# Group normalisation in 32 tiles: the next tile's mean read ahead of this tile's variance on VectorE

## The chip, the cores and the metric

The kernel runs on one core of a Trainium2 chip. The metric is the device time of one execution in microseconds (us). Times quoted are medians of several executions. One core gives no second core to compare with, so "fast" below means only that an execution lay within 1.5% of the fastest of its kernel. The span of a profile is the time from its first to its last instruction; it is some 1.7 us shorter than the device time.

## The reference

```python
# x: (128, 1024, 32, 16) bf16; g, b: (1024,) bf16; 32 groups of 32 channels
xr  = x.reshape(B, 32, 32, H, W)
mu  = xr.mean(axis=(2, 3, 4), keepdims=True)
var = ((xr - mu) ** 2).mean(axis=(2, 3, 4), keepdims=True)
xn  = (xr - mu) / sqrt(var + 1e-5)
return xn.reshape(B, C, H, W) * g[None, :, None, None] + b[None, :, None, None]
```

The input has 134 MB and so has the output. Both pass through the DMA once.

## The kernel before

A row of a tile is one group of one sample: 32 channels of 512 elements. A tile is 128 such rows, 4 MiB; there are 32 tiles and six buffers for them. Loads and stores all go out on one queue. For each tile `i`:

- `L(i)` loads it; `M(i)` has TensorE add up its 32 slices with an identity matrix, into PSUM (the memory that TensorE writes its sums to);
- `R(i)` reads those sums on VectorE and makes the (negative) mean;
- `Q(i)` squares the tile, less its mean, in four passes on ScalarE, each with a sum;
- `V(i)` makes variance, 1/sqrt, scale and bias: small VectorE steps with one ScalarE square root among them;
- `A(i, lo, hi)` scales slices `lo` to `hi` in place on VectorE, one instruction each;
- `S(i)` stores it.

```python
def chain(key, inst):            # keeps the instructions of one engine in program order
    prev = last.get(key)
    if prev is not None:
        tc.add_manual_dep(inst.ins, prev.ins.name, nosync, reason="pipeline order")
    last[key] = inst
    return inst

# ... (constants; the casts of gamma and beta on VectorE, which are in no chain)

def R(i):                        # mean of tile i: waits for M(i)
    ...
    chain("dve", nc.vector.tensor_scalar(out=jd[:], in0=st["ps"][:], scalar1=-inv_n, ...,
                                         accum_out=negmean[:]))

def V(i):                        # ... four VectorE steps and this one on ScalarE:
    chain("act", nc.scalar.activation(out=rstd[:], in_=var[:], func=ACT.Sqrt, bias=eps_t[:], ...))

# ...
M(0)
R(0)
for i in range(NT):
    Q(i)
    V(i)
    if i + 1 < NT:
        M(i + 1)
    A(i, 0, A_HEAD)              # A_HEAD = 12 of 32 slices
    if i + 1 < NT:
        R(i + 1)                 # the next mean stands between two parts of the scaling
    A(i, A_HEAD, KC)
    S(i)
    j = i + AHEAD                # AHEAD = 5; L(j) reuses the buffer of tile i-1
    if UPFRONT <= j < NT:
        L(j)
```

Of the kernel before, what the change touches and what calls it, by code (L numbers as in the profile page):

```python
# [18 lines left out]
AHEAD = 5  # L19
MM_FREE = 512  # L20
SQ_FREE = 4096
A_HEAD = 12


@with_exitstack
def kernel(
# [16 lines left out]
    NT = B0 // NS  # L43
    KC = C // G
# [25 lines left out]
    def chain(key, inst):  # L70
# [5 lines that stand above are left out]
# [3 lines left out]
    def L(i):  # L79
        xt = xpool.tile([P, F], BF16, name="xt")  # L80
        chain("sp", nc.sync.dma_start(out=xt[:], in_=x_v[i]))
        state[i] = {"xt": xt}
# [32 lines left out]
    def M(i):  # L115
        st = state[i]
        ps = pspool.tile([P, MMN], F32, name="ps")
        for k in range(NMM):
            chain(
                "pe",  # L120
                nc.tensor.matmul(  # L121
                    out=ps[:],
                    lhsT=eye[:],
                    rhs=st["xt"][:, k * MMN : (k + 1) * MMN],
                    start=(k == 0),
                    stop=(k == NMM - 1),
                ),
            )
        st["ps"] = ps

    def R(i):
        st = state[i]
        negmean = spool.tile([P, 1], F32, name="negmean")
        jd = jpool.tile([P, MMN], BF16, name="jd")
        chain(
            "dve",
            nc.vector.tensor_scalar(  # L137
                out=jd[:],
                in0=st["ps"][:],
                scalar1=-inv_n,  # L140
                scalar2=None,
                op0=ALU.mult,
                op1=ALU.add,
                accum_out=negmean[:],
            ),
        )
        st["negmean"] = negmean

    def Q(i):
        st = state[i]  # L150
        sq = spool.tile([P, NSQ], F32, name="sq")
        for k in range(NSQ):
            ja = jpool.tile([P, SQ_FREE], BF16, name="ja")
            chain(
                "act",
                nc.scalar.activation(  # L156
                    out=ja[:],
                    in_=st["xt"][:, k * SQ_FREE : (k + 1) * SQ_FREE],
                    func=ACT.Square,
                    bias=st["negmean"][:],  # L160
                    scale=1.0,
                    accum_out=sq[:, k : k + 1],
                ),
            )
        st["sq"] = sq

    def V(i):
        st = state[i]
        var = spool.tile([P, 1], F32, name="var")
        jv = spool.tile([P, NSQ], F32, name="jv")  # L170
        chain(
            "dve",
            nc.vector.tensor_scalar(  # L173
                out=jv[:],
                in0=st["sq"][:],
                scalar1=inv_n,
                scalar2=None,
                op0=ALU.mult,
                op1=ALU.add,
                accum_out=var[:],  # L180
            ),
        )
        rstd = spool.tile([P, 1], F32, name="rstd")
        chain(
            "act",
            nc.scalar.activation(  # L186
                out=rstd[:], in_=var[:], func=ACT.Sqrt, bias=eps_t[:], scale=1.0
            ),
        )
        chain("dve", nc.vector.reciprocal(out=rstd[:], in_=rstd[:]))  # L190
        scl = spool.tile([P, KC], F32, name="scl")
        bia = spool.tile([P, KC], F32, name="bia")
        chain(
            "dve",
            nc.vector.tensor_scalar(  # L195
                out=scl[:], in0=gam[:], scalar1=rstd[:], scalar2=None, op0=ALU.mult
            ),
        )
        chain(
            "dve",  # L200
            nc.vector.scalar_tensor_tensor(  # L201
                out=bia[:],
                in0=scl[:],
                scalar=st["negmean"][:],
                in1=bet[:],
                op0=ALU.mult,
                op1=ALU.add,
            ),
        )
        st["scl"], st["bia"] = scl, bia  # L210

    def A(i, lo, hi):
        st = state[i]
        xt = st["xt"]
        for k in range(lo, hi):
            chain(
                "dve",
                nc.vector.tensor_scalar(  # L218
                    out=xt[:, k * HW : (k + 1) * HW],
                    in0=xt[:, k * HW : (k + 1) * HW],  # L220
                    scalar1=st["scl"][:, k : k + 1],
                    scalar2=st["bia"][:, k : k + 1],
                    op0=ALU.mult,
                    op1=ALU.add,
                ),
            )

    def S(i):
        chain("sp", nc.sync.dma_start(out=o_v[i], in_=state[i]["xt"][:]))
        state.pop(i)  # L230
# [2 lines left out]
    R(0)  # L233
    for i in range(NT):
        Q(i)
        V(i)
        if i + 1 < NT:
            M(i + 1)
        A(i, 0, A_HEAD)
        if i + 1 < NT:  # L240
            R(i + 1)
        A(i, A_HEAD, KC)
        S(i)
        j = i + AHEAD
        if UPFRONT <= j < NT:
            L(j)
# [30 lines left out]
```

## Time and profile before

| | before |
|---|---|
| time | 732.8 us (732.75 to 732.81, 3 runs) |
| ScalarE, VectorE, TensorE busy | 68%, 52%, 40% |
| one tile after another | every 21.28 us |
| bytes moved, both ways | 367 GB/s over the span |

The page of the kernel before. The first row is the busy share of the DMA in 40 slices of the span, in tenths; the second what it moved; then the chain that ended last (the work followed back from the last instruction, at each step to what released it), by engine.

```profile
DMA  9998599999999999999999999999999999934555
GB/s 377 431 437 364 229 385 390 403 402 377 397 404 402 373 402 401 402 375 402 402 374 402 402 402 372 403 402 402 373 420 385 378 400 398 401 145 202 229 229 229
...
ACT 68%; DVE 25%; DMA 4%; issue 1%; ACTq 0%; DVEq 0%
```

The DMA seems full for 35 slices, but for a dip at the fifth and sixth, and half empty for the last five. Yet the chain hardly runs through it. The waits say why (engine, what it was about to do, for whom it waited: us in all, times, longest):

```profile
DVE jv L173 <- ACT ja L156: 293.1, 32, 15.4
ACT ja L156 <- DVE jd L137: 199.1, 32, 30.1
```

ScalarE's squares (`ja`) wait for VectorE's mean (`jd`), and VectorE's variance (`jv`) waits for ScalarE's squares. That is a loop. The timeline shows one turn of it; each row has start, duration, engine and operation, and in brackets the idle time before it and who ended it.

```profile
303.12 0.16 DVE L173 TENSOR_SCALAR_CACHE_REDUCE jv<-sq 128x4 f32<-128x4 f32 x1 [8.96 <-ACT ja L156]
...
304.41 3.97 DVE L218 TENSOR_SCALAR xt<-xt,scl,bia 128x512 bf16<-128x512 bf16 x12
308.29 0.68 DVE L137 TENSOR_SCALAR_CACHE_REDUCE jd<-ps 128x512 bf16<-128x512 f32 x1
...
309.07 3.71 ACT L156 ACTIVATE ja<-xt,negmean 128x4096 bf16<-128x4096 bf16 x1 [5.46 <-DVE jd L137]
...
324.40 0.16 DVE L173 TENSOR_SCALAR_CACHE_REDUCE jv<-sq 128x4 f32<-128x4 f32 x1 [8.96 <-ACT ja L156]
```

Squares take 15.3 us, the variance steps 1.3, twelve slices 3.97, the mean 0.75: together about 21.3 us, and the turn from 303.12 to 324.40 is 21.28. In each turn ScalarE idles 5.46 us and VectorE 8.96. No engine is full. The Trainium skill ("Perfetto Trace Analysis", Optimization Strategy) has one look for the gaps and for what ends them; here that names the loop at once, where the busy shares name nothing.

Windows in time show that the DMA follows the loop (columns: window, its length, then busy us and number of instructions for PE, PEld, DVE, ACT and POOL, then the TensorE clock, the DMA's busy share and GB/s):

```profile
300.00:400.00 100.00, 40.78 (x149) 15.94 (x146) 58.69 (x194) 71.16 (x42) 0.00 (x0) 0.72 0.96 396
...
645.00:656.00 11.00, 0.59 (x3) 0.10 (x1) 10.91 (x34) 6.44 (x3) 0.00 (x0) 0.75 0.00 0
656.00:666.00 10.00, 0.00 (x0) 0.00 (x0) 0.71 (x5) 9.06 (x7) 0.00 (x0) 0.50 0.98 419
666.00:677.00 11.00, 0.00 (x0) 0.00 (x0) 10.96 (x35) 6.17 (x3) 0.00 (x0) 0.50 0.01 1
```

In the middle it is busy 0.96 of the time; near the end a store takes 10 us and is followed by 11 us of nothing.

### The profile page before, as it was taken

The numbers are of one execution on the slowest core, as the hardware profiler recorded it, in microseconds if no ns is written. First come the engines' busy times: TensorE is split into PE (matmuls) and PEld (weight loads), VectorE is DVE, ScalarE is ACT, GpSimd is POOL, SyncE is SP. The second block draws the span as 40 slices with busy tenths as digits, with TensorE's granted clock in tenths as the row PEclk, the third lists the DMA queues.
The fourth block names the chain that finished last, engine by engine and source line by source line (L and its number), as shares of the span: only waits on it lengthen the run. The fifth ranks groups of instructions, "written<-read, shape, count | busy, mean of one in ns | idle before, by whom it ended". The sixth has DMA issues, their size and how long they took to land.

```text
span 731.1 us, 3814 instructions
## 1 busy us (share of the span) xinstructions
PE 288.9 (40%) x1024; PEld 113.1 (15%) x1024; DVE 379.8 (52%) x1252; ACT 497.5 (68%) x290; POOL 0.5 (0%) x5
## 2 busy tenths in 40 slices
PE   2874532455543334445323455433344443330000
PEld 0331110122111111112111122111111111110000
DVE  0034466654446665444566544456654445665443
ACT  0267876666787666678766667876666787666670
POOL 0000000000000000000000000000000000000000
PEclk9997656666667667776667766677767776675555
DMA  9998599999999999999999999999999999934555
GB/s 377 431 437 364 229 385 390 403 402 377 397 404 402 373 402 401 402 375 402 402 374 402 402 402 372 403 402 402 373 420 385 378 400 398 401 145 202 229 229 229
DMA packets 9622, 268.70 MB, mean 368 GB/s; under 512 B 1408, under 2 KB 1408, under 8 KB 1408
## 3 DMA queue, kind: packets, MB, share of 16 engines
q1 hardware_dynamic: 9216, 268.44, 88.7%
q8 instruction: 8, 0.13, 0.1%
q14 instruction: 14, 0.11, 0.0%
q10 hardware_dynamic: 384, 0.02, 0.0%
HBM read 134.23 MB, written 134.22 MB: 367 GB/s over the span
## 4 chain that ended last, share of the span: by engine, by line
ACT 68%; DVE 25%; DMA 4%; issue 1%; ACTq 0%; DVEq 0%
ACT ja L156 67%; DVE xt L218 18%; DVE jd L137 3%; DMA bet_b<-in_b_dram 3%; DMA xt<-in_x_dram 2%; ACT rstd L186 1%; DVE bia L201 1%; DVE scl L195 1%; DVE jv L173 1%; DVE rstd L190 1%; ACTq L156 0%; DVEq L272 0%; DVE bet L113 0%
## 5 line engine op out<-in xcount | busy, mean ns | idle before, releaser
L156 ACT ACTIVATE ja<-xt,negmean 128x4096 bf16<-128x4096 bf16 x128 | 474.7, 3708 | 202.2 <-DVE jd L137 199.1
L121 PE MATMUL ps<-xt,eye 128*128 128x512 bf16 x1024 | 288.9, 453 | 356.7 <-DMA xt<-in_x_dram 343.9
L218 DVE TENSOR_SCALAR xt<-xt,scl,bia 128x512 bf16<-128x512 bf16 x1024 | 335.9, 403 | 1.2
L121 PEld LDWEIGHTS <-eye 128*128 128x128 bf16 x1024 | 113.1, 113 | 532.0 <-DMA xt<-in_x_dram 343.4
L173 DVE TENSOR_SCALAR_CACHE_REDUCE jv<-sq 128x4 f32<-128x4 f32 x32 | 5.0, 157 | 293.1 <-ACT ja L156 293.1
L156 ACT ACTIVATION_READ_ACCUMULATOR ja<-xt,negmean 128x1 f32 x128 | 23.9, 187 | 0.0
L137 DVE TENSOR_SCALAR_CACHE_REDUCE jd<-ps 128x512 bf16<-128x512 f32 x32 | 21.8, 680 | 0.0
L186 ACT ACTIVATE rstd<-var,eps_t 128x1 f32<-128x1 f32 x32 | 9.4, 294 | 7.4 <-DVE jv L173 7.4
L112 DVE CAST gam<-gam_b 128x32 f32<-128x32 bf16 x1 | 0.2, 181 | 26.9 <-DMA gam_b<-in_g_dram 26.9
L190 DVE RECIPROCAL rstd<-rstd 128x1 f32<-128x1 f32 x32 | 5.3, 164 | 11.6 <-ACT rstd L186 11.6
L201 DVE SCALAR_TENSOR_TENSOR bia<-scl,negmean,bet 128x32 f32<-128x32 f32 x32 | 8.0, 251 | 1.1
L195 DVE TENSOR_SCALAR scl<-gam,rstd 128x32 f32<-128x32 f32 x32 | 7.7, 242 | 1.1
L173 DVE DVE_READ_ACCUMULATOR jv<-sq 128x1 f32 x32 | 2.6, 83 | 0.0
L137 DVE DVE_READ_ACCUMULATOR jd<-ps 128x1 f32 x32 | 2.5, 79 | 0.0
L113 DVE CAST bet<-bet_b 128x32 f32<-128x32 bf16 x1 | 0.2, 181 | 3.4 <-DMA bet_b<-in_b_dram 3.4
L90 ACT ACT_TABLE_LOAD x1 | 1.3, 1283 | 0.8 <-PEq L261 0.8
L88 DVE MEMSET eps_t<- 128x1 f32 x1 | 0.1, 59 | 0.9 <-PEq L261 0.9
L101 POOL TENSOR_SCALAR_AFFINE_SELECT eye<-ones_b 128x128 bf16<-128x128 bf16 x1 | 0.3, 293 | 0.7 <-DVE ones_b L99 0.7
L90 ACT ACTIVATE warm<-eps_t 128x1 f32<-128x1 f32 x1 | 0.2, 202 | 0.0
L99 DVE MEMSET ones_b<- 128x128 bf16 x1 | 0.2, 165 | 0.0
L261 POOL MEMSET const-bfloat16-1.0<- 128x1 bf16 x1 | 0.1, 101 | 0.0
L261 POOL MEMSET const-uint8-127<- 128x1 uint8 x1 | 0.1, 101 | 0.0
(2 smaller groups left out, 0.2 us busy)
## 6 DMA issues: line engine op xcount, KB each, us to landing
xt<-in_x_dram SPq DMA_DIRECT2D x32, 4096.0 KB, 21.9
out_dram<-xt SPq DMA_DIRECT2D x32, 4096.0 KB, 12.1
gam_b<-in_g_dram ACTq DMA_DIRECT2D x4, 2.0 KB, 15.7
bet_b<-in_b_dram ACTq DMA_DIRECT2D x4, 2.0 KB, 17.1
```

The lines of the kernel that those rows point to most:

```text
L90: chain("act", nc.scalar.activation(out=warm[:], in_=eps_t[:], func=ACT.Sqrt))
L99: nc.vector.memset(ones_b[:], 1.0)
L101: nc.gpsimd.affine_select(out=eye[:], in_=ones_b[:], pattern=[[-1, P]], compare_op=ALU.is_equal, fill=0.0, base=0, channel_multiplier=1,)
L121: nc.tensor.matmul(out=ps[:], lhsT=eye[:], rhs=st["xt"][:, k * MMN : (k + 1) * MMN], start=(k == 0), stop=(k == NMM - 1),),
L137: nc.vector.tensor_scalar(out=jd[:], in0=st["ps"][:], scalar1=-inv_n, scalar2=None, op0=ALU.mult, op1=ALU.add, accum_out=negmean[:],),
L156: nc.scalar.activation(out=ja[:], in_=st["xt"][:, k * SQ_FREE : (k + 1) * SQ_FREE], func=ACT.Square, bias=st["negmean"][:], scale=1.0, acc ...
L173: nc.vector.tensor_scalar(out=jv[:], in0=st["sq"][:], scalar1=inv_n, scalar2=None, op0=ALU.mult, op1=ALU.add, accum_out=var[:],),
L186: nc.scalar.activation(out=rstd[:], in_=var[:], func=ACT.Sqrt, bias=eps_t[:], scale=1.0),
L190: chain("dve", nc.vector.reciprocal(out=rstd[:], in_=rstd[:]))
L195: nc.vector.tensor_scalar(out=scl[:], in0=gam[:], scalar1=rstd[:], scalar2=None, op0=ALU.mult),
L201: nc.vector.scalar_tensor_tensor(out=bia[:], in0=scl[:], scalar=st["negmean"][:], in1=bet[:], op0=ALU.mult, op1=ALU.add,),
L218: nc.vector.tensor_scalar(out=xt[:, k * HW : (k + 1) * HW], in0=xt[:, k * HW : (k + 1) * HW], scalar1=st["scl"][:, k : k + 1], scalar2=st[ ...
```

## The change

The intent: ScalarE shouldn't wait for VectorE's scaling. The next tile's mean depends only on its load and its matmuls, so it can be read while ScalarE squares this tile and VectorE is idle. `R(i + 1)` moves ahead of `V(i)`; with nothing left to put between two parts of the scaling, a tile is scaled in one go. No instruction is added or removed.

```diff
-A_HEAD = 12
...
-    def A(i, lo, hi):
+    def A(i):
...
-        for k in range(lo, hi):
+        for k in range(KC):
...
     for i in range(NT):
         Q(i)
-        V(i)
         if i + 1 < NT:
             M(i + 1)
-        A(i, 0, A_HEAD)
-        if i + 1 < NT:
             R(i + 1)
-        A(i, A_HEAD, KC)
+        V(i)
+        A(i)
         S(i)
```

## The prediction

> **What bounds the kernel now.** A loop of waits between two engines, with the DMA close behind. The timeline (300 to 350 us) repeats every 21.28 us: ScalarE squares a tile in four passes (15.3 us), VectorE makes its variance, scale and bias (1.3), scales 12 of 32 slices (3.97), only then reads the next tile's mean (0.7), and that mean releases ScalarE. The waits view shows ScalarE idle 199.1 us for that mean, 32 times, about 5.5 us each and 30 the first time. The chain that ended last says the same: ACT 68%, DVE 25%. No engine is full: ACT 68%, DVE 52%, PE 40%. Loads arrive about two tiles early; PE's 343.9 us of waits for loads are run-ahead.
>
> The DMA moves 8.39 MB per tile. In one-us windows a pair (store, then load) is under way for about 20.2 of the 21.28 us, then nothing for 1.1 to 1.2 us until the next store is issued. In the tail (from 645 us) stores come every 21.28 us and the DMA is idle half the time.
>
> **What the change does.** No instruction is added or removed. The mean of tile i+1 is read while ScalarE squares tile i, when VectorE sits idle 9 us. Removed from the loop: 3.97 us of scaling, 0.7 of mean, and the scale and bias. What is left between two squares is the variance wait (0.23) and the square root (0.3). ScalarE could then do a tile in 15.9 us; VectorE needs 12.5, PE about 8.7.
>
> So the limit passes to the DMA. A transfer of 4.19 MB takes about 9.8 us (six loads at the start land 9.8 apart, mostly), and a pair 20.2. The Trainium skill ("DMA: Bandwidth & Descriptors", Queues, rings and completion order) says that one engine's ring is consumed in order; the trace agrees (store lands 12.1 us after issue, the load behind it 21.9). Its specifications give about 358 GB/s as a core's HBM limit; this trace holds 394 for hundreds of us, so I use the trace.
>
> **Where the gain comes from** (estimates from these durations):
> - Start: store 1 goes out at 75.5 us, not 81.4, and ends an idle DMA: 6 us.
> - Middle: 26 pairs at 20.2 instead of 21.28: about 28 us. ScalarE first gains on the loads, uses up their lead by about tile 11, and then waits for them, so its gain stops there.
> - Tail: the last five stores queue back to back, about 10 us apart, not 21.28: about 45 us.
>
> Sum: DMA starts at 76; 26 pairs x 20.2 = 525; five stores x 9.8 = 49; landing 1.5; launch 1.7. That is 653. I add a few us for load-to-store turnarounds, which before never met back to back: **657 us, 643 to 682**. Chances: faster by over 2% 0.96, within 2% 0.03, slower 0.01.
>
> **Cost of the move.** The variance of tile i now stands behind the mean of i+1 in VectorE's order, so it waits for load i+1. Once loads are late, store i can't go before load i+1 is in. Five tiles of lookahead should hide this; I give it nothing.
>
> **What would show it right.** ScalarE's waits for the mean: near zero for the first 10 tiles, then about 4.5 us each, for the load and the matmuls behind it. Store issues 15.9 us apart at first, then about 20.2. DMA share near full from 76 us to the end, 410 to 420 GB/s; no half-idle tail. Busy times of ACT and DVE unchanged. Chain: mostly DMA.
>
> **What would make it wrong.** Stores and loads really overlapping might run slower (400 GB/s gives about 675), or turnarounds cost 1 us each. If the coupling of store i to load i+1 starves the DMA queue, the middle stays near 21 us and only start and tail pay: about 685.

## The result, and the profile after

| | before | after |
|---|---|---|
| time | 732.77 us (4 runs) | 643.48 us (642.11 to 644.48, 4 runs) |
| ratio | | 0.878 (0.8763 to 0.8797) |
| ScalarE, VectorE, TensorE busy | 68%, 52%, 40% | 77%, 59%, 44% |
| bytes moved over the span | 367 GB/s | 419 GB/s |

A ratio is the mean time of one kernel's fast runs over that of the other's of the same rounds, so it isn't quite the ratio of the medians. The page after:

```profile
DMA  9999699999999999999999999999999999999986
GB/s 370 442 430 425 297 392 424 424 427 433 438 426 427 434 441 417 426 436 439 421 432 431 439 425 427 434 434 429 429 436 438 426 429 436 435 429 427 435 345 270
...
DMA 63%; ACT 22%; PE 8%; DVE 5%; issue 1%; DVEq 0%; SPq 0%
```

The chain now runs through the DMA. The half-empty tail has gone, and the middle moves 431 GB/s (windows below) where it moved 396. The waits that answer to the loop (`L155` and `L136` are the same squares and mean; line numbers moved):

```profile
ACT rstd L185 <- DVE jv L172: 90.1, 32, 4.9
...
ACT ja L155 <- DVE jd L136: 30.0, 1, 30.0
```

ScalarE waits for a mean only once, at the very start. It still waits, for 90.1 us, but under another name: its square root (`rstd`) waits for the variance of its own tile. The timeline shows the reason:

```profile
415.04 8.82 PE L120 MATMUL ps<-xt,eye 128*128 128x512 bf16 x32 [11.59 <-DMA xt<-in_x_dram]
...
423.89 0.69 DVE L136 TENSOR_SCALAR_CACHE_REDUCE jd<-ps 128x512 bf16<-128x512 f32 x1 [8.08 <-PE ps L120]
...
424.51 0.15 DVE L172 TENSOR_SCALAR_CACHE_REDUCE jv<-sq 128x4 f32<-128x4 f32 x1
...
424.70 0.29 ACT L185 ACTIVATE rstd<-var,eps_t 128x1 f32<-128x1 f32 x1 [4.92 <-DVE jv L172]
```

The variance (424.51) stands behind the next tile's mean (423.89), which waits for that tile's matmuls, which waited for its load. So the wait that the trace gives to VectorE comes from the DMA, three steps back.

```profile
300.00:400.00 100.00, 48.56 (x167) 18.98 (x169) 59.29 (x195) 78.47 (x46) 0.00 (x0) 0.71 1.00 431
400.00:500.00 100.00, 47.70 (x162) 18.62 (x165) 59.27 (x195) 78.07 (x46) 0.00 (x0) 0.71 1.00 431
```

The windows of after have the DMA full for hundreds of us. A load is now issued every 19.70 us (187.91 to 562.26 us in the timeline of issues, 19 steps).

Where the 89.7 us of the two traces' spans came from, cut at two marks that both have: the issue of the second store (the first moment from which the changed DMA is never empty for long), and the start of the last tile's matmuls (its load is in):

| | before | after | gained | predicted |
|---|---|---|---|---|
| start to the issue of store 1 | 81.4 | 75.1 | 6.3 | 6 |
| to the last load in | 555.5 | 517.2 | 38.3 | 28 |
| to the end | 94.2 | 49.1 | 45.1 | 45 |
| sum | 731.1 | 641.4 | 89.7 | 79, less 4 of margin |

The third row starts at these rows of the timelines, the first two before, the others after; they show where ScalarE was when the last load was in, and how the changed kernel ends:

```profile
628.25 3.71 ACT L156 ACTIVATE ja<-xt,negmean 128x4096 bf16<-128x4096 bf16 x1 [5.45 <-DVE jd L137]
636.87 8.73 PE L121 MATMUL ps<-xt,eye 128*128 128x512 bf16 x32 [12.64 <-DMA xt<-in_x_dram]
...
581.85 3.69 ACT L155 ACTIVATE ja<-xt,negmean 128x4096 bf16<-128x4096 bf16 x1
592.25 3.17 PE L120 MATMUL ps<-xt,eye 128*128 128x512 bf16 x7 [11.45 <-DMA xt<-in_x_dram]
601.25 0.69 DVE L136 TENSOR_SCALAR_CACHE_REDUCE jd<-ps 128x512 bf16<-128x512 f32 x1 [8.09 <-PE ps L120]
602.26 3.69 ACT L155 ACTIVATE ja<-xt,negmean 128x4096 bf16<-128x4096 bf16 x1
617.58 0.16 DVE L172 TENSOR_SCALAR_CACHE_REDUCE jv<-sq 128x4 f32<-128x4 f32 x1 [4.00 <-ACT ja L155]
618.87 10.42 DVE L217 TENSOR_SCALAR xt<-xt,scl,bia 128x512 bf16<-128x512 bf16 x32
```

### The profile page after: what moved, and what is told of

It reads as the page before. It is cut to its first block, busy times and chain, and to the rows that moved or that the text cites. A ratio compares the mean times of both kernels' runs of the same rounds, so it can differ in the third digit from the quotient of the medians.

```text
span 641.4 us, 3795 instructions
## 1 busy us (share of the span) xinstructions
PE 285.3 (44%) x1004; PEld 112.8 (18%) x1024; DVE 380.2 (59%) x1252; ACT 494.1 (77%) x290; POOL 0.5 (0%) x5
## 4 chain that ended last, share of the span: by engine, by line
DMA 63%; ACT 22%; PE 8%; DVE 5%; issue 1%; DVEq 0%; SPq 0%
DMA out_dram<-xt 30%; DMA xt<-in_x_dram 29%; ACT ja L155 21%; PE ps L120 8%; DVE xt L217 3%; DMA bet_b<-in_b_dram 3%; DVE jd L136 1%; DVE jv L172 0%; ACT rstd L185 0%; DVE scl L194 0%; DVE bia L200 0%; DVE rstd L189 0%; DVEq L269 0%; DVE bet L112 0%; SPq L80 0%
## 5 line engine op out<-in xcount | busy, mean ns | idle before, releaser
L155 ACT ACTIVATE ja<-xt,negmean 128x4096 bf16<-128x4096 bf16 x128 | 474.2, 3704 | 33.1 <-DVE jd L136 30.0
L120 PE MATMUL ps<-xt,eye 128*128 128x512 bf16 x1004 | 285.3, 451 | 315.9 <-DMA xt<-in_x_dram 302.7
L136 DVE TENSOR_SCALAR_CACHE_REDUCE jd<-ps 128x512 bf16<-128x512 f32 x32 | 22.0, 689 | 156.7 <-PE ps L120 149.0
L185 ACT ACTIVATE rstd<-var,eps_t 128x1 f32<-128x1 f32 x32 | 9.4, 294 | 90.1 <-DVE jv L172 90.1
L155 ACT ACTIVATION_READ_ACCUMULATOR ja<-xt,negmean 128x1 f32 x128 | 23.8, 186 | 0.0
L136 DVE DVE_READ_ACCUMULATOR jd<-ps 128x1 f32 x32 | 2.6, 82 | 0.0
```

What stands on the lines that cost most here:

```text
L120: nc.tensor.matmul(out=ps[:], lhsT=eye[:], rhs=st["xt"][:, k * MMN : (k + 1) * MMN], start=(k == 0), stop=(k == NMM - 1),),
L155: nc.scalar.activation(out=ja[:], in_=st["xt"][:, k * SQ_FREE : (k + 1) * SQ_FREE], func=ACT.Square, bias=st["negmean"][:], scale=1.0, acc ...
```

## The experiments

Three questions were open. Is the loop, and its exit behind twelve slices, really what was cured (e1, e2)? Are the three rows of that table three separate gains (e3, e4)? And is the DMA the new limit, and what does a pair of store and load cost on it (e5 to e7)? Then four runs tried to use the answer.

### e1: no slice before the mean, but the mean still behind the variance

```diff
-A_HEAD = 12
+A_HEAD = 0
```

> The old order with the first part of the scaling cut from 12 slices to 0: the next mean is read after the variance but before any slice is scaled. Theory A (what mattered was getting the mean out from behind the 12 slices; after that the DMA limits): the engine loop is 15.3+1.3+0.75, about 17.4 us, shorter than the 19.5 us that a store and a load take, so the time is that of the changed kernel within 1%: 641 to 649 us. Rival B (the mean must also stand ahead of the variance, because the 1.6 us of loop left over counts): 31 x 1.6 = 50 us slower than the changed kernel, about 690 us.

Measured: 645.44 us, ratio 0.881 to before (0.8796 to 0.8825). Theory A holds. Ordering the mean ahead of the variance, which the change is named for, isn't what earns the gain. Taking it out from behind the slices is. In e1 ScalarE waits 111.4 us for means and 7.4 us for variances; the changed kernel has it the other way (30.0 and 90.1). Its waits:

```profile
ACT ja L156 <- DVE jd L137: 111.4, 32, 30.1
...
ACT rstd L186 <- DVE jv L173: 7.4, 32, 0.2
```

The sum is nearly the same, 118.8 and 120.1 us: e1's own loop is longer (its early stores are 17.28 us apart, those of the changed kernel 15.7), but that only takes from the time that ScalarE would otherwise wait for loads. The one difference left that I see is at the start: store 1 leaves at 77.2 us and not 75.1, and the whole is 2.0 us longer.

### e2: six slices before the mean

```diff
-A_HEAD = 12
+A_HEAD = 6
```

> The old order with 6 slices before the next mean. If the loop between ScalarE and VectorE is what bounded the kernel before, its period is 21.28 - 6 x 0.327 = 19.3 us, and as that is near the DMA's 19.5 us the whole is about 670 us (660 to 680), with stores about 19.4 us apart all the way to the end. If the DMA alone had set the 21.28 us, nothing would change in the middle: 715 to 733 us.

Measured: 672.64 us, ratio 0.918 (0.9166 to 0.9194). Stores leave every 19.34 us (311.39 to 582.22 us, 14 steps), up to the last. The loop was the bound of the kernel before: six slices less take 1.94 us off each turn, as estimated (6 x 0.327), and 31 turns of that are 60.1 us, the whole gain. Here the loop's 19.34 us and the DMA's 19.7 are nearly level, yet the kernel is 29 us slower than the changed one. The next two runs say why.

### e3 and e4: the new order in the last tiles only, and everywhere but there

```diff
     for i in range(NT):
         Q(i)
+        if NEW(i):                    # e3: i >= 27    e4: i < 27
+            if i + 1 < NT:
+                M(i + 1)
+                R(i + 1)
+            V(i)
+            A(i, 0, KC)
+        else:
+            ...                       # the old order
```

> The new order for tiles 27 to 31 only (after the last load is issued), the old order before. Theory A (the long tail of the kernel before is a backlog of 3 to 4 loaded but unsquared tiles; the new order saves 5.4 us for each of them, only four steps are left): about 711 us. Rival B (the sum of the prediction, where the tail by itself is worth 45 us): about 688 us.

> The new order for tiles 0 to 26, the old order for 27 to 31. Theory A (the middle drains the backlog, so no long tail is left whichever order it runs in): 645 to 652 us. Rival B (terms add; the tail's 45 us are lost): about 688 us.

Measured: e3 710.45 us (ratio 0.9696, 0.9682 to 0.971), e4 648.80 us (0.8854, 0.8841 to 0.8868). Both fit theory A and both rule out the sum. Fixing only the tail wins 22.3 us of the 45 in the table's third row. Fixing everything but the tail wins 83.9 of 89. So the rows show where the time was seen to go, not what each part is worth alone.

The tail of the kernel before was a backlog. When the last load was in, at 636.9 us, ScalarE was still in the squares of tile 28 (begun at 628.25 us), with 29, 30 and 31 to come, at 21.28 us each. In the changed kernel the last load was in at 592.3 us and ScalarE was in tile 30 (begun at 581.85 us). The faster middle had let ScalarE catch up with the loads, and with no backlog there is no tail to speed up. In e2 the loop runs about as fast as the DMA, so ScalarE hardly catches up: when the last load was in, at 595.4 us, it was in the squares of tile 29, and the rest took 75.6 us and not 49.1. Those 26.5 us are most of its 29.

### e5: the transfers alone

All compute is taken out, and stores and loads keep their order (a wrong result).

```diff
     for i in range(NT):
-        Q(i)
-        ...
-        A(i)
         S(i)
         j = i + AHEAD
         if UPFRONT <= j < NT:
             L(j)
```

> All 32 loads and 32 stores in the same order on the same queue with no compute between (a wrong result on purpose: the input comes out). If the DMA bounds the changed kernel's middle, this takes 64 transfers x 9.75 to 9.85 plus about 5 us: 628 to 640 us, and its pair of store and load takes 19.5 to 19.7 us, as in the changed kernel (425 to 433 GB/s). If the changed kernel's middle is set by something else (ScalarE, PE), it is much shorter: below 600 us.

Measured (one run, with a profile): 633.97 us. A load is issued every 19.67 us (101.39 to 553.81 us, 23 steps), against 19.70 in the changed kernel. The DMA limits the changed kernel's middle, and all of its compute adds only 9.5 us to the transfers. Windows of e5 (no TensorE in it, so the columns are DVE, ACT, POOL, clock, DMA share, GB/s):

```profile
300.00:400.00 100.00, 0.00 (x0) 0.00 (x0) 0.00 (x0) 1.00 1.01 433
400.00:500.00 100.00, 0.00 (x0) 0.00 (x0) 0.00 (x0) 1.00 1.00 432
```

### e6: the same transfers, each pair begun on an empty queue

```diff
     for i in range(NT):
+        k = i + AHEAD - 1
+        if UPFRONT - 1 <= k < NT:     # store i waits until load i+4 has landed
+            nc.vector.tensor_copy(out=state[i]["xt"][:, 0:1], in_=state[k]["xt"][:, 0:1])
         S(i)
```

> The same transfers, but store i is held back by a one-column copy until load i+4 has landed, so that a store and the load behind it always start on an empty queue, as in the kernel before (a wrong result on purpose). Theory A (why I took 20.2 us for a pair: the filling of an empty queue is in that number, and a queue that never empties doesn't pay it): bytes are under way for about 20.2 us per pair, and with the wait for landing and the new issue the pair comes every 21.5 to 22.5 us, about 690 to 715 us in all. Rival B (a pair takes 19.5 us of transfer however it starts): under way 19.5 us, period 20.5 to 21.3.

Measured (one run, with a profile): 698.27 us; a pair every 22.11 us (114.39 to 622.83 us, 23 steps).

```profile
300.00:400.00 100.00, 0.62 (x4) 0.00 (x0) 0.00 (x0) 1.00 0.93 381
400.00:500.00 100.00, 0.78 (x5) 0.00 (x0) 0.00 (x0) 1.00 0.92 377
```

Theory A holds for the period (21.5 to 22.5 was expected) and rules out rival B; its 20.2 us under way is too short. The store of one pair is issued at 312.70 us. By the packet records of the kept trace (start, length and size of every DMA packet, which the views here only add up) its first packet starts at 313.54 us, the last packet of its load ends at 334.37, and the next pair's first packet starts at 335.84: 20.8 us under way, then 1.5 us of nothing. (The 20.2 had been read from windows, which book a packet where it starts and so miss most of the last one, 1.2 us long.) In e5 the queue never empties and a pair costs 19.67. Emptying it costs 22.11 - 19.67 = 2.4 us a pair: some 1.5 us in which nothing moves, and some 0.9 us in which the DMA moves less than it can. The packet records show where: most 32 KB packets take about 1.21 us, but 657 of the 8192 take over 1.3 in e6, 658 in the kernel before, 147 in the changed kernel and 127 in e5. Nearly all those of e6 start 9 to 13 us after a store's issue, where the load follows the store; all packets' time above 1.21 us comes to 427 us in e6 and 48 in e5, which over 16 engines and the 27 held-back pairs is 0.9 us a pair. The kernel before has as many, though its queue is only nearly empty between pairs: in its middle no stop of all sixteen engines is over 0.8 us, where the windows had seemed to show 1.1 to 1.2. Why these packets are slow is not shown.

### e7: half the squares

```diff
-        for k in range(NSQ):
+        for k in range(NSQ // 2):     # in V, two sums are added in place of four
```

> The changed kernel with two of the four squaring passes (a wrong result on purpose): ScalarE needs 8.2 us for a tile, not 15.9. If the DMA bounds the middle, the middle's period stays 19.5 to 19.7 us and only the start and the end shorten: 620 to 634 us. If ScalarE (77% busy, the busiest engine on the page) bounds it, the gain is of the order of 100 us or more.

Measured (one run, with a profile; wrong): 636.42 us, 2 us above the range that I gave but nowhere near 100 us of gain. ScalarE's busy time halves to 250.8 us. The middle stays at 433 GB/s and 19.65 us a load (103.49 to 496.54 us, 20 steps). ScalarE, the busiest compute engine on the changed kernel's page, doesn't limit its middle. The 7 us fit the start: stores begin at 51.8 us, and from 70 to 76 us, where the changed kernel's DMA has a gap, this one's is full (1.01).

### e8 to e11: the gaps at start and end

The changed kernel's DMA has two gaps left:

```profile
70.00:76.00 6.00, 0.13 (x1) 0.00 (x0) 5.65 (x18) 5.94 (x5) 0.00 (x0) 0.82 0.16 66
...
626.00:628.00 2.00, 0.00 (x0) 0.00 (x0) 2.00 (x8) 0.00 (x0) 0.00 (x0) 0.50 0.04 16
628.00:630.00 2.00, 0.00 (x0) 0.00 (x0) 1.29 (x5) 0.00 (x0) 0.00 (x0) 0.50 0.08 33
```

At the start the first mean stands behind two casts, of gamma and beta, which wait for small loads until 31.6 us. At the end nothing can be stored until the last tile is through. e8 is the changed kernel again, as a yardstick; e9 moves the casts; e10 cuts the last tile's load and store in four; e11 does both.

```diff
# e9
-    nc.vector.tensor_copy(out=gam[:], in_=gam_b[:])
-    nc.vector.tensor_copy(out=bet[:], in_=bet_b[:])
...
     M(0)
     R(0)
+    nc.vector.tensor_copy(out=gam[:], in_=gam_b[:])
+    nc.vector.tensor_copy(out=bet[:], in_=bet_b[:])
# e10: PARTS are the four quarters of a row
+        for lo, hi in PARTS if i == NT - 1 else [(0, F)]:
+            chain("sp", nc.sync.dma_start(out=xt[:, lo:hi], in_=x_v[i][:, lo:hi]))
...
+        for lo, hi in PARTS:          # the last tile
+            A(i, lo // HW, hi // HW)
+            chain("sp", nc.sync.dma_start(out=o_v[i][:, lo:hi], in_=xt[:, lo:hi]))
```

> The changed kernel unaltered, as the yardstick for the three runs beside it: 642 to 645 us.

> The changed kernel with the two small casts of gamma and beta moved behind the first mean, so that the first squaring needn't wait until 31.6 us for a small load it has no use for. First square at about 22.7 us instead of 32.3. Theory A (the DMA bounds all from store 1 on, so only the DMA's idle 5 us at 70 to 75 us can be won): 5 us faster than the changed kernel, 638 to 639 us. Rival B (the whole 9.6 us are won because every later step moves up): 634 us. Rival C (nothing, since the end is set by the last load's chain and the queue was full by then anyway): 643 us.

> The changed kernel with the last tile loaded and stored in four parts. Theory A (at the end the DMA idles some 6 us before the last store, since matmuls, mean, squares and scaling of the last tile stand after its load): the parts start the matmuls and the last store early, and 5 to 7 us are won: 636 to 639 us. If the end is DMA-bound already: 643 us.

> Both edits. If the two idle stretches are separate, the gains add: 632 to 634 us, no better than the transfers alone (634 us), which is the floor of this order of transfers. Otherwise about 638 us.

Measured: e8 643.59 us, e9 642.96, e10 643.84, e11 643.01; ratios to before 0.878, 0.8781, 0.8786 and 0.8777, with intervals that overlap. All three edits missed.

For e9 the timeline gives the reason: the edit wasn't in the program that ran.

```profile
27.87 0.18 DVE L231 CAST gam<-gam_b 128x32 f32<-128x32 bf16 x1 [26.77 <-DMA gam_b<-in_g_dram]
31.43 0.18 DVE L232 CAST bet<-bet_b 128x32 f32<-128x32 bf16 x1 [3.38 <-DMA bet_b<-in_b_dram]
31.52 0.68 DVE L134 TENSOR_SCALAR_CACHE_REDUCE jd<-ps 128x512 bf16<-128x512 f32 x1
```

The casts come later in the source and still run ahead of the mean; they are in no chain, and the order of the source doesn't bind them. So e9 tested nothing, and e11 is e10 over again.

e10 did what its edit says: the four last parts are issued between 616.7 and 624.8 us, where the changed kernel issues its last store at 629.3. It ends at the same time all the same. Windows of e10:

```profile
624.00:630.00 6.00, 0.00 (x0) 0.00 (x0) 0.42 (x2) 0.00 (x0) 0.00 (x0) 0.50 0.98 416
630.00:632.00 2.00, 0.00 (x0) 0.00 (x0) 0.00 (x0) 0.00 (x0) 0.00 (x0) 0.50 0.66 279
632.00:634.00 2.00, 0.00 (x0) 0.00 (x0) 0.00 (x0) 0.00 (x0) 0.00 (x0) 0.50 0.35 147
634.00:636.00 2.00, 0.00 (x0) 0.00 (x0) 0.00 (x0) 0.00 (x0) 0.00 (x0) 0.50 0.18 78
636.00:638.00 2.00, 0.00 (x0) 0.00 (x0) 0.00 (x0) 0.00 (x0) 0.00 (x0) 0.50 0.06 25
638.00:640.00 2.00, 0.00 (x0) 0.00 (x0) 0.00 (x0) 0.00 (x0) 0.00 (x0) 0.50 0.06 25
```

The share is a mean over 16 DMA engines, and 0.06 is what one of sixteen would make. The engines run out of work one by one over ten microseconds, and the last ends where it ended before. The gap in the changed kernel is then to be read anew: from 626 to 630 us its share is 0.04 to 0.08, so most engines idled while about one was still at work. An earlier last store only gives the others their work sooner. The packet records of the kept traces bear this out. In e10 the engines write their last bytes one after another, from 630.3 to 639.8 us. In the changed kernel eleven engines are through with store 30 by 624.4 us and idle until 630.2, but the last is through with it at 630.47 and goes straight on with store 31, which all sixteen end between 639.9 and 640.2. So no earlier issue could have helped that engine. Which one it is, and why it lags, these profiles don't show.

### e12: the casts in the chain

```diff
     M(0)
     R(0)
+    chain("dve", nc.vector.tensor_copy(out=gam[:], in_=gam_b[:]))
+    chain("dve", nc.vector.tensor_copy(out=bet[:], in_=bet_b[:]))
```

> The casts of gamma and beta really behind the first mean on VectorE: in e9 the order didn't change, because the casts stood in no chain and were placed ahead all the same; here they are chained. First square at about 22.7 us, store 1 at about 66 us, so no idle DMA at 70 to 75 us. Theory A (the DMA, and in it the engine that ends last, works without a pause from store 1 to the end, so just the idle 5 to 6 us are won): 637 to 639 us. Rival B (all 9.6 us are won): 634 us. Rival C (nothing): 643 us.

Measured: 636.68 us (635.96 to 637.36), correct, ratio 0.869 to before (0.8678 to 0.8702). Beside the changed kernel's 643.59 in e8, also timed against before, that is 6.9 us less. The first mean runs at 21.96 us, store 1 leaves at 65.5 us, and the DMA has no gap:

```profile
21.96 0.69 DVE L134 TENSOR_SCALAR_CACHE_REDUCE jd<-ps 128x512 bf16<-128x512 f32 x1 [20.86 <-PE ps L118]
...
27.90 0.18 DVE L231 CAST gam<-gam_b 128x32 f32<-128x32 bf16 x1 [5.24 <-DMA gam_b<-in_g_dram]
...
70.00:76.00 6.00, 3.17 (x15) 1.25 (x13) 5.89 (x20) 5.97 (x3) 0.00 (x0) 1.00 1.00 431
```

Store 1 moved by 9.6 us and the end by about 7: only the DMA's idle time could be won, and a microsecond or two more than its 5 to 6 us, but not the 9.6. The rest fits the cost of restarting an emptied queue that e6 shows: between 84 and 97 us, behind its gap, the changed kernel has 55 packets of over 1.3 us (53 when run again as e8), 1.9 us of excess over sixteen engines, and e12 has none there. This kernel beats both others. It is 2.7 us from the transfers alone (e5, a single run of which the state is unknown).

## Why the prediction was right

- **The loop between ScalarE and VectorE bounds the kernel.** Right. Shown by e2, which moves it by six slices and gets 31 times their time, and by e1.
- **The limit passes to the DMA.** Right. e5 has the same 19.7 us with no compute, and e7 halves the busiest engine's work without touching the middle.
- **Start: 6 us.** Measured 6.3. Right.
- **Middle: "26 pairs at 20.2 instead of 21.28: about 28 us".** Measured 38.3. This term was mis-sized. A pair on a full queue costs 19.7 us; the 20.2 was read (by windows) from pairs that began on a nearly empty queue, and e6 shows that such pairs take longer because of that. With 19.7 the term is 26 x 1.58 = 41 us, 3 more than was measured; some 2 of these 3 are the slow packets at 84 to 97 us, which e12 hasn't. The margin that I put on top, "a few us for load-to-store turnarounds", went the wrong way too: back to back, they cost nothing that shows. Together these put 657 where 643.5 was measured, at the low edge of the range: half a microsecond inside it, with one of the four runs (642.11) below. That the range held is in part luck.
- **The Trainium skill has the number I needed.** I quoted the 358 GB/s of "DMA: Bandwidth & Descriptors" (Specifications) and set it aside. That figure is a share for two cores that stream at once. "HBM Reference" (Specifications) says that a core streaming alone measures about 425 GB/s, bounded by its 16 DMA engines. The 8.39 MB of a pair at 425 GB/s are an estimate of 19.74 us from that page; e5 measured 19.67 and moved 425 GB/s over its whole span.
- **Tail: 45 us.** Measured 45.1, but not for a reason of its own. e3 and e4 show that the reordered tail is worth 22 us if the middle stays slow and 5 if the middle is fast. The prediction did say that ScalarE uses up the loads' lead, and that is the step that removes the tail; to list it as a third, separate gain was wrong. That "the last five stores queue back to back, about 10 us apart" is not how they are issued (562.7, 575.0, 593.2, 613.6 and 629.3 us), but it is how the engine that lags moves them: records that close a transfer stand 9.68 us apart at 591.7, 601.4, 611.1, 620.8, 630.5 and 640.2 us (taken as one engine's by their spacing), the last load and five stores with no pause, the 49 us forecast. The last tile's own steps, which let the other engines pause, take as long by chance: matmuls 9.0, mean 1.0, squares 15.3, variance steps 1.3, scaling 10.4, store to the end 12.1, in all 49.1.
- **What the trace would show.** ScalarE was to have used up the loads' lead by about tile 11; its square roots are 15.7 us apart up to tile 9 and further apart from tile 10 on. The early stores are 15.7 us apart (15.9 forecast), the DMA is full, the chain is mostly DMA: all so, but at 431 GB/s in the middle and not 410 to 420, which is the mis-sized pair again. "ScalarE's waits for the mean ... then about 4.5 us each" had the size about right (4.2 on average from tile 10 to 30, 4.9 at the longest) and the name wrong: the variance stands behind the mean, so ScalarE waits at its square root.
- **"The variance of tile i now stands behind the mean of i+1".** I gave this cost nothing, and e1, which keeps the variance ahead, is no faster. That it is the five tiles of lookahead that hide it is argued; no run shortened them.

## What to carry to other kernels

When two engines wait for each other in turn and neither is full, add up one turn of the loop, and ask which instruction stands in it only because of its place in the order; moving that one may cost nothing, as here. Then size the next limit in the state in which the new kernel will run it: a DMA rate read where the queue empties every turn is too low for a queue that stays full. And don't add up gains by stretches of the timeline, since a tail can be the backlog of the middle.

## What the Trainium skill lacked or had wrong

- "DMA: Bandwidth & Descriptors" (Specifications, and the note that for HBM to SBUF transfers "the HBM side (~358) binds") is too low for one core alone: the changed kernel and the transfers alone held 431 to 433 GB/s for hundreds of us, close to that page's 435 GB/s fabric ceiling. The figure is meant for two cores at once, and the same page's table of measured transfers, of one core, has 425 GB/s at 16 MB. "HBM Reference" has it right (about 425; e5's mean is 425).
- No page says what it costs to let the queue run empty between large transfers. Here it was 2.4 us per pair (22.11 against 19.67 us), some 1.5 of it a stop and some 0.9 slower packets. "DMA: Bandwidth & Descriptors" (Anatomy of one DMA) gives a fixed 2.0 us for a DMA of the other issue path (GpSimd's), of the same order.
- No page says that a mix of loads and stores on a full queue runs as fast as loads alone: e5 held 431 GB/s in the mix and 428 to 431 in its second and third slices.
- No page that I read gives a size for how far apart the 16 engines of one queue can end a long plain stream; in e10 it was ten microseconds (the busy share fell from 0.98 before 630 us to 0.06 at 636), and an earlier last store won nothing.
